# The second expert's first weights: packed values folded in by 64-row tiles and kept in HBM

## Chip, cores and metric

The kernel runs on one core of one Trainium2 chip. The metric is the time of one execution in device microseconds. Before the change it is 1086.9 us, the median of 3 runs (1085.64 to 1087.13).

## What is computed

```python
def sm_attn(qq, kk, vv):            # scale = 1/sqrt(64)
    a = softmax(scale * qq @ kk.T)
    return a @ vv
p_packed = sm_attn(p, k, v)         # 32 packed rows per head
x = sm_attn(q, p_packed, p_packed)  # 4 batches, 8 heads, 576 tokens, 64 wide
x = x as 2304 tokens x 512
out = 0
for e in range(4):                  # experts, weights w1[e] 512x1024, w2[e] 1024x512
    out += prob[:, e] * (relu(x @ w1[e]) @ w2[e])
out = (s * relu(out @ w_in)**2 + b) @ w_out
```

The second attention ends in a product of its weights a2 (tokens by 32 packed rows of each of 8 heads) with the packed values, and expert e begins with a product by w1[e]. The kernel multiplies the packed values into w1[e] first ("folds" them), so that per batch and expert one matrix of 256 rows (8 heads x 32) by 1024 columns stands in place of w1[e], and the expert reads a2 directly.

## The kernel before, in words

Numbers that must stay exact are kept in two parts, a high part (rounded to the fp32r type) and a low part (the rest), and each product is three matmuls: low x high, high x high, high x low.

After the first attention of batch 0 the main loop runs over 256 units, `ua`: expert e, batch bi, half hf of the batch's tokens, and one of 8 column blocks f. One turn i of the loop is called step i here. A batch is SB = 16 steps, an expert 64. In step i the loop first calls `run(i)`, which issues whatever was woven in at that step with `at(step, fn, ...)`, then `m1` for unit i + 2 (a2 times the folded first weights, L777, into a bank `h`; its relu is split by ScalarE, L798, and VectorE, L800), then `m2` for unit i (times w2, L823, into `acc`). So the order on every engine is written out by hand by the step numbers in the `at` calls (L1241 to L1284), and each engine works its list in order. SyncE (SP) issues nearly all DMAs, also in list order; a DMA that has to wait holds up those behind it.

Expert 0's weights are folded batch by batch out of the packed values `ptw` by `fold_w1`. Three forms of fold exist before the change:

- Expert 1 (the second): at steps 49 and 50 `pair_p` (L509) splits `ptw` into `ptph` and `ptpl`, laid out so that two batches lie on one 128 x 128 block. `load_w1` and `split_w1` bring and split w1[1] in four column groups. `fold_pair` (L613) then makes, for a pair of batches j, a column group c and x, six matmuls of 128 x 128 by 256 columns (L621), and ACT (L629) and DVE (L633) evict the two halves into `w1p` tiles in SBUF. j = 0 stands at steps 57 to 64, j = 1 at steps 89 to 96.
- Experts 2 and 3: at steps 91 and 93 `heads_p` (L526) gathers `pth` out of `ptph` and `ptpl`, eight POOL copies. `load_w1b`, `split_w1b` and `fold_heads` (L570) work on 64-row tiles: for a column half n, a row group gi and x, each of the three products is two matmuls with 64 rows and 512 columns, one for each half z of the partitions (L575), and ACT (L581) and DVE (L582) evict two banks into `w1o` tiles. `store_heads` (L590) writes them to `w1p_dram` in HBM, two DMAs of 512 KB a call. This is done for all four batches at once. `load_w1p` (L602) brings each batch's part back later, for each n and gi in four DMAs of 32 partitions.

What the tiles come from matters for the waits. `w1p` for even batches comes from 4 buffers of the pool `keep`, which expert 0 uses for its own folded weights until its last m1; `w1o` and the raw weights share 7 slots (`take`, `give`); the banks of a fold come from `ps_m`, 2 buffers; raw second weights come from 3 buffers, `load_w2` (L646) at steps 54 to 61 and `split_w2` (ACT L654, POOL L657) at steps 57 to 64 for expert 1.

The core of `fold_heads`, which the change calls for expert 1 too:

```python
for i, (a, w) in enumerate(((1, 0), (0, 0), (0, 1))):
    for z in range(2):
        r = slice(64 * z, 64 * z + 64)
        nc.tensor.matmul(
            ps[z], lhsT=pth[a][r, gi, x, :], rhs=w1s[e, n, gi][w][r, x, :],
            start=(i == 0), stop=(i == 2),
        )
```

Of the kernel before, what the change touches and what calls it, by code (L numbers as in the profile page):

```python
# [19 lines left out]
def attention_experts_mlp_kernel(  # L20
# [431 lines left out]
    def load_w1(e, c):  # L452
        if e == 0:
            t = keep.tile([P, KB, 256], F32, tag="w1", bufs=4, name=f"w1_{e}{c}")
        else:
            w1q[e, c], t = take([P, KB, 256], F32, f"w1r_{e}{c}")
        nc.sync.dma_start(
            out=t, in_=w1[e, :, c * 256 : (c + 1) * 256].rearrange("(r a) f -> a r f", a=P)
        )
        w1_t[e, c] = t  # L460
# [34 lines left out]
    def w1p_tile(e, bi, c):  # L495
        pool = wodd if bi % 2 else keep
        t = pool.tile([P, 2, G, 256], F32R, tag="w1p", bufs=4, name=f"w1p_{e}{bi}{c}")
        w1p[e, bi, c] = t[:, 0], t[:, 1]
        return w1p[e, bi, c]


    ptp, w1s = {}, {}
# [3 lines left out]
        for e in range(2, E)  # L506
    }

    def pair_p(j):  # L509
        if j == 0:  # L510
            for i, x in enumerate("hl"):
                ptp[i] = wf.tile([P, G, 2, 2, P], F32R, tag="ptp", bufs=2, name="ptp" + x)
        hi, lo = (ptp[i][:, :, :, j, :] for i in range(2))
        for bi in (0, 1):
            for y in range(2):
                r = slice(64 * y, 64 * y + 64)
                x = y ^ bi
                src = ptw[2 * j + bi][:, :, r]
                nc.scalar.activation(hi[:, :, x, r], src, AF.Copy)
                nc.gpsimd.tensor_tensor(  # L520
                    out=lo[:, :, x, r], in0=src, in1=f32(hi[:, :, x, r]), op=ALU.subtract
                )
# [3 lines left out]
    def heads_p(i):  # L526
        t = pth[i] = wf.tile([P, G, 2, P], F32R, tag="pth", bufs=2, name=f"pth{i}")
        for z in range(2):
            r = slice(64 * z, 64 * z + 64)
            for gi in range(G):  # L530
                nc.gpsimd.tensor_copy(
                    t[r, gi].rearrange("a x (j h r) -> a x j h r", j=2, h=2),
                    ptp[i][r, gi].rearrange("a x j (h z r) -> a z x j h r", h=2, z=2)[:, z ^ gi],
                )

    def split_w1(e, c, i):
        if i == 0:
            w1q["h", e, c], hi = take([P, KB, 256], F32R, f"w1h_{e}{c}")
            w1s[e, c] = (
                hi, keep.tile([P, KB, 256], F32R, tag="w1", bufs=4, name=f"w1l_{e}{c}")  # L540
            )
        hi, lo, raw = (x[:, 2 * i : 2 * i + 2] for x in (*w1s[e, c], w1_t[e, c]))
        nc.scalar.activation(hi, raw, AF.Copy)
        nc.vector.tensor_tensor(out=lo, in0=raw, in1=f32(hi), op=ALU.subtract)
        if i == 1:
            give(w1q[e, c])
# [61 lines left out]
    def w1p_block(e, bi, f, gi, x):  # L608
        if e == 1:
            return w1p[e, bi, f // 2][x][:, gi, (f % 2) * P : (f % 2 + 1) * P]  # L610
        return w1p[e, bi, f // 4, gi][:, x, (f % 4) * P : (f % 4 + 1) * P]

    def fold_pair(e, j, c, x):  # L613
        t = ps_m.tile([P, G, 256], F32, tag="m", name=f"pp1_{e}{j}{c}{x}")
        ph, pl = (ptp[i][:, :, :, j, :] for i in range(2))
        if j == 1 and x == 1:
            give(w1q["h", e, c])
        for gi in range(G):
            wh, wl = (w[:, 2 * gi + x] for w in w1s[e, c])
            for n, (a, w) in enumerate(((pl, wh), (ph, wh), (ph, wl))):  # L620
                nc.tensor.matmul(  # L621
                    t[:, gi, :], lhsT=a[:, gi, x, :], rhs=w, start=(n == 0), stop=(n == 2)
                )
        if x == 0:
            for bi in (2 * j, 2 * j + 1):
                w1p_tile(e, bi, c)
# [810 lines left out]
```

## Time and profile before

| | |
|---|---|
| median of 3 runs | 1086.9 us |
| the profiled execution | 1086.37 us |
| its span, first to last instruction | 1084.3 us |
| TensorE (PE) busy | 99% of the span |
| VectorE (DVE), ScalarE (ACT), GpSimd (POOL) busy | 62%, 42%, 18% |
| DMA moved | 170.23 MB, mean 157 GB/s |

The times are of the profiled execution; its span leaves out what lies before the first and after the last instruction. PE is the matmul stream, PEld the loading of its stationary operand, which runs beside it. SPq is the issue of DMAs by SyncE. A row of a timeline gives start, duration, engine, line, operation, output and input by the program's names, shapes and count, and in brackets the idle time before it and what ended that. Because matmuls overlap in the pipeline, the distance between starts, not the duration, is what one costs.

### The profile page before, as it was taken

Reading aid. Unit: us, or ns where it says so; the run is one execution under the profiler, and the core shown is the slowest. Engines: PE = TensorE matmul, PEld = TensorE weight load, DVE = VectorE, ACT = ScalarE, POOL = GpSimd, SP = SyncE. Lnnn points to the kernel's source line nnn. Section 1 sums busy time; section 2 is a strip of 40 time slices with the busy share of each in tenths; the row PEclk is TensorE's granted clock in tenths of the full one; section 3 lists DMA queues with packets and bytes.
Section 4 is the critical chain, followed back from the end, with each engine's and each line's share of the span. In section 5 each row is a group of like instructions: output and inputs, shape, how many; then the busy total and the mean of one; then the engine's idle time right before and its main releaser. Section 6 shows DMA issues by size and latency. Waiting matters only on the chain.

```text
span 1084.3 us, 16975 instructions
## 1 busy us (share of the span) xinstructions
PE 1069.9 (99%) x6263; PEld 914.9 (84%) x6263; DVE 676.4 (62%) x1298; ACT 450.1 (42%) x1014; POOL 195.3 (18%) x193
## 2 busy tenths in 40 slices
PE   8999999999999999999999999989999999999998
PEld 5777778888887888888888888878888888889887
DVE  7885754675575456465457645589845765775554
ACT  3533333553444343333435766665631332343111
POOL 1520212221110131010131122234201120210000
PEclk9999999999999999999999999999999999999999
DMA  9763320133036775575676242336856555665532
GB/s 285 177 114 69 69 89 1 40 107 115 32 103 223 226 216 159 182 216 172 207 192 191 73 126 88 134 139 242 330 187 216 185 208 172 217 209 184 183 113 88
DMA packets 102685, 170.23 MB, mean 157 GB/s; under 512 B 48185, under 2 KB 64825, under 8 KB 102603
## 3 DMA queue, kind: packets, MB, share of 16 engines
q1 hardware_dynamic: 101755, 168.04, 49.0%
q10 hardware_dynamic: 848, 1.11, 0.3%
q8 instruction: 50, 0.82, 0.3%
q14 instruction: 32, 0.26, 0.1%
HBM read 122.72 MB, written 46.40 MB: 156 GB/s over the span
## 4 chain that ended last, share of the span: by engine, by line
PE 92%; DVE 2%; ACT 2%; DMA 1%; issue 1%; SPq 1%; POOL 1%; ACTq 0%; DVEq 0%; POOLq 0%
PE acc L823 34%; PE h L777 18%; PE o L1018 18%; PE h L982 15%; PE pp L575 1%; PE pp L621 1%; DMA v<-in_v_dram 1%; PE pw L473 1%; PE pv L308 1%; PE s L375 0%; ACT xs L926 0%; PE tr L290 0%; PE warm L1068 0%; DMA q<-in_q_dram 0%; DVE xs L927 0%
## 5 line engine op out<-in xcount | busy, mean ns | idle before, releaser
L777 PEld LDWEIGHTS h<-a,w1p 128*128 128x128 f32 x1536 | 226.7, 188 | 33.2 <-issue 9.9
L777 PE MATMUL h<-a,w1p 128*128 128x320 f32 (+1 forms) x1536 | 250.6, 298 | 1.4 <-DVE rest L800 0.9
L1018 PE MATMUL o<-wo,gg 128*128 128x512 f32 x864 | 224.7, 394 | 2.0 <-DVE gg L950 2.0
L800 DVE SCALAR_TENSOR_TENSOR hl<-h,hh 128x256 fp32r<-128x256 f32 x256 | 107.9, 421 | 187.4 <-ACT rest L798 102.9
L982 PE MATMUL h<-xs,wop 128*128 128x384 f32 x1008 | 203.8, 338 | 1.5 <-DVE xt L844 1.5
L823 PE MATMUL acc<-w2l,hh 128*128 128x512 f32 x512 | 201.4, 393 | 0.5 <-POOL w2l L657 0.5
L823 PE MATMUL acc<-w2h,hh 128*128 128x512 f32 x512 | 201.5, 393 | 0.0
L823 PE MATMUL acc<-w2h,hl 128*128 128x512 f32 x512 | 200.3, 391 | 0.0
L982 PEld LDWEIGHTS h<-xs,wop 128*128 128x128 f32 x1008 | 180.9, 188 | 15.4 <-DVE xt L844 1.7
L1018 PEld LDWEIGHTS o<-wo,gg 128*128 128x128 f32 x864 | 160.1, 188 | 27.7 <-DVE gg L950 2.9
L798 ACT ACTIVATE hh<-h 128x256 fp32r<-128x256 f32 x256 | 97.3, 380 | 171.5 <-PE h L777 168.8
L823 PEld LDWEIGHTS acc<-w2h,hl 128*128 128x128 f32 x512 | 96.2, 188 | 21.7
L823 PEld LDWEIGHTS acc<-w2l,hh 128*128 128x128 f32 x512 | 96.4, 188 | 15.4 <-POOL w2l L657 0.7
L823 PEld LDWEIGHTS acc<-w2h,hh 128*128 128x128 f32 x512 | 96.4, 188 | 13.3
L936 ACT ACTIVATE yy<-yy 128x768 f32<-128x768 f32 x48 | 40.3, 839 | 112.9 <-DVE yy L1002 112.9
L1002 DVE TENSOR_TENSOR yy<-h,uv 128x384 f32<-128x384 f32 x96 | 51.0, 552 | 47.5 <-PE h L982 47.3
L946 ACT ACTIVATE gg<-yy,b_sb 128x768 fp32r<-128x768 f32 x48 | 44.8, 934 | 37.5 <-DVE yy L939 36.3
L950 DVE SCALAR_TENSOR_TENSOR gg<-yy,b_sb,gg 128x768 fp32r<-128x768 f32 x48 | 53.7, 1120 | 1.8 <-ACT gg L946 1.8
L657 POOL TENSOR_TENSOR w2l<-w2r,w2h 128x512 fp32r<-128x512 f32 x24 | 31.1, 1294 | 127.9 <-ACT w2h L654 104.5
L939 DVE SCALAR_TENSOR_TENSOR yy<-yy,s_sb 128x768 f32<-128x768 f32 x48 | 51.8, 1080 | 0.0
L1002 DVE TENSOR_TENSOR uv<-h,uv 128x384 f32<-128x384 f32 x48 | 26.4, 553 | 38.2 <-PE h L982 38.0
L1034 DVE TENSOR_TENSOR o_sb<-o,o_sb 128x512 f32<-128x512 f32 (+1 forms) x55 | 36.9, 673 | 16.7 <-PE o L1018 16.7
(399 smaller groups left out, 1146.9 us busy)
## 6 DMA issues: line engine op xcount, KB each, us to landing
xs<-xs_dram SPq DMA_DIRECT2D x63, 768.0 KB, 4.3
w1p_dram<-w1o SPq DMA_DIRECT2D x32, 512.0 KB, 3.7
w1p<-w1p_dram SPq DMA_DIRECT2D x128, 128.0 KB, 4.3
xs_dram<-xs SPq DMA_DIRECT2D x21, 768.0 KB, 3.5
w1r<-in_moe_w_dram SPq DMA_DIRECT2D x12, 512.0 KB, 4.8
w2r<-in_moe_w_dram SPq DMA_DIRECT2D x24, 256.0 KB, 3.8
out_dram<-o_sb SPq DMA_DIRECT2D x17, 256.0 KB, 2.0
v<-in_v_dram SPq DMA_DIRECT2D x8, 512.0 KB, 5.6
```

The lines of the kernel that those rows point to most:

```text
L777: nc.tensor.matmul(t[:, : width(bi, hf)], lhsT=w1p_block(e, bi, f, gi, w), rhs=a2[bi][:, x, gi, part(bi, hf)], start=(n == 0), stop=(n == ...
L798: nc.scalar.activation(hi, src, AF.Relu)
L800: nc.vector.scalar_tensor_tensor(out=lo, in0=src, scalar=0.0, in1=f32(hi), op0=ALU.max, op1=ALU.subtract)
L823: nc.tensor.matmul(acc[j], lhsT=x, rhs=w, start=(f == 0 and n == 0), stop=(g == NF - 1 and n == 2),)
L936: nc.scalar.activation(y, y, AF.Relu)
L939: nc.vector.scalar_tensor_tensor(out=y, in0=y, scalar=s_sb, in1=y, op0=ALU.mult, op1=ALU.mult)
L946: nc.scalar.activation(t[:, 0], y, AF.Identity, bias=b_sb)
L950: nc.vector.scalar_tensor_tensor(out=t[:, 1], in0=y, scalar=b_sb, in1=f32(t[:, 0]), op0=ALU.add, op1=ALU.subtract)
L982: nc.tensor.matmul(ps, lhsT=w[:, a, col], rhs=x[:, z, m, :], start=(n == 0), stop=(n == 3 * HK - 1),)
L1002: nc.vector.tensor_tensor(out=dst, in0=ps, in1=src, op=ALU.add)
L1018: nc.tensor.matmul(o_acc[i], lhsT=lhsT, rhs=w, start=(f == 0 and n == 0), stop=(f == FG - 1 and n == 2),)
L1034: nc.vector.tensor_tensor(out=dst[:, c], in0=acc[:, c], in1=dst[:, c], op=ALU.add)
```

## The change

Expert 1 takes the way of experts 2 and 3. `fold_pair`, `pair_p`, `split_w1` and `w1p_tile` go; `w1p_dram` gets an entry for expert 1; `load_w1` is left for expert 0 alone. The packed values are gathered anew: `heads_pick` copies them from `ptw` by POOL, 16 copies of 64 partitions x 32 at step 33 and 16 at step 41, into `p_pick`, a free part of the tile that holds the rows of the expert probabilities; `heads_p`, at step 48, then splits them by one ACT and one DVE instruction. `heads_p` at steps 91 and 93 goes. For expert 1, `split_w1b` stands at steps 50 to 57, `fold_heads` one step later, `store_heads` two steps later, one call in every step; `load_w1p` for its first batch at steps 57, 58, 61 and 62, for the others as experts 2 and 3 have it (the first four steps of the batch before).

```diff
-        if e == 0:
-            t = keep.tile([P, KB, 256], F32, tag="w1", bufs=4, name=f"w1_{e}{c}")
-        else:
-            w1q[e, c], t = take([P, KB, 256], F32, f"w1r_{e}{c}")
+        t = keep.tile([P, KB, 256], F32, tag="w1", bufs=4, name=f"w1_{e}{c}")
...
-        for e in range(2, E)
+        for e in range(1, E)
     }
...
+    def heads_pick(j):
+        t = p_pick.rearrange("a (g x j h r) -> a g x j h r", g=G, x=2, j=2, h=2)
         for z in range(2):
             for gi in range(G):
+                for h in range(2):
+                    for x in range(2):
+                        r = 64 * h + 32 * (z ^ gi)
+                        nc.gpsimd.tensor_copy(
+                            t[half(z), gi, x, j, h], ptw[2 * j + (x ^ h)][half(z), gi, r : r + 32]
+                        )
...
+    def heads_p():
+        for i in range(2):
+            pth[i] = wf.tile([P, G, 2, P], F32R, tag="pth", bufs=2, name=f"pth{i}")
+        hi, lo = (pth[i].rearrange("a g x c -> a (g x c)") for i in range(2))
+        nc.scalar.activation(hi, p_pick, AF.Copy)
+        nc.vector.tensor_tensor(out=lo, in0=p_pick, in1=f32(hi), op=ALU.subtract)
...
     def w1p_block(e, bi, f, gi, x):
-        if e == 1:
-            return w1p[e, bi, f // 2][x][:, gi, (f % 2) * P : (f % 2 + 1) * P]
         return w1p[e, bi, f // 4, gi][:, x, (f % 4) * P : (f % 4 + 1) * P]
...
                 for c in range(4):
-                    if ne == 1 and nb % 2 == 0:
-                        for x in range(2):
-                            at(s0 + 9 + 2 * c + x, fold_pair, ne, nb // 2, c, x)
-                for c in range(4):
                     n, gi = divmod(c, 2)
-                    if ne > 1:
-                        d = c if nb else (6, 7, 13, 14)[c]
+                    if ne:
+                        d = c if nb else ((6, 7, 13, 14) if ne > 1 else (9, 10, 13, 14))[c]
                         at(s0 + d, load_w1p, ne, nb, n, gi)
-                    if bi != B - 1 or ne < 2:
+                    if bi != B - 1:
                         continue
                     for x in range(2):
                         k = 2 * c + x
-                        if n:
+                        if ne == 1:
+                            d = s0 + 2 + k
+                        elif n:
                             d = s0 + 2 * k - 7
...
                         if x == 0:
-                            at(d - 4, load_w1b, ne, n, gi)
+                            at(max(d - 4, s0) if ne == 1 else d - 4, load_w1b, ne, n, gi)
                         at(d, split_w1b, ne, n, gi, x)
                         at(d + 1, fold_heads, ne, n, gi, x)
-                        at(d + 3, store_heads, ne, n, gi, x)
+                        at(d + (2 if ne == 1 else 3), store_heads, ne, n, gi, x)
                 if bi == B - 1:
-                    for c in range(4 if ne == 1 else 0):
-                        at(s0 + (0, 1, 5, 7)[c], load_w1, ne, c)
-                        for i in range(2):
-                            at(s0 + 3 + 2 * c + i, split_w1, ne, c, i)
...
-        for j in range(2):
-            at((B - 1) * SB + 1 + j, pair_p, j)
-            at((B + 1) * SB + 11 + 2 * j, heads_p, j)
+        at(2 * SB + 1, heads_pick, 0)
+        at(2 * SB + 9, heads_pick, 1)
+        at((B - 1) * SB, heads_p)
```

The order of the instructions shows three places. First SP's list from expert 1's first weights to the raw weights of the last layers (w1r: raw first weights, w2r: raw second weights, wi0raw: raw weights of the last layers), before:

```order
L457 DMA w1r_2506<-in_moe_w_dram 128x4x256
L646 DMA w2r_2532<-in_moe_w_dram 128x512
L457 DMA w1r_2558<-in_moe_w_dram 128x4x256
L646 DMA w2r_2560<-in_moe_w_dram 128x512
L646 DMA w2r_2585<-in_moe_w_dram 128x512
...
L646 DMA w2r_2772<-in_moe_w_dram 128x512
L678 DMA wi0raw<-in_moe_w_in_dram 128x4x256
```

and with the change, from the third block of second weights to the last load of expert 1's first batch:

```order
L595 DMA w2r_2702<-in_moe_w_dram 128x512
L573 DMA w1p_2724<-w1p_dram_90 32x1024 x4
L561 DMA w1p_dram_90<-w1o_2692 128x1024
L561 DMA w1p_dram_90<-w1o_2695 128x1024
L595 DMA w2r_2751<-in_moe_w_dram 128x512
L573 DMA w1p_2772<-w1p_dram_90 32x1024 x4
...
L595 DMA w2r_2845<-in_moe_w_dram 128x512
L573 DMA w1p_2864<-w1p_dram_90 32x1024 x4
L595 DMA w2r_2873<-in_moe_w_dram 128x512
L627 DMA wi0raw<-in_moe_w_in_dram 128x4x256
L573 DMA w1p_2894<-w1p_dram_90 32x1024 x4
```

Where only second weights stood, the last stores (L561) and the loads of the first batch (L573) now stand between them.

On PE, the first fold of expert 1 with the m1 (h) behind it, at step 57 of the kernel before:

```order
L621 MATMUL pp_1000_2607<-w1h_2452,ptpl 128x256
L621 MATMUL pp_1000_2607<-w1h_2452,ptph 128x256
L621 MATMUL pp_1000_2607<-w1l_2453,ptph 128x256
L621 MATMUL pp_1000_2607<-w1h_2452,ptpl 128x256
L621 MATMUL pp_1000_2607<-w1h_2452,ptph 128x256
L621 MATMUL pp_1000_2607<-w1l_2453,ptph 128x256
L777 MATMUL h_2630<-a_3_2198,w1p_2219 128x256 x3
L777 MATMUL h_2630<-a_3_2198,w1p_2221 128x256 x3
```

and the first fold of expert 1 with the change, at step 51:

```order
L546 MATMUL pp_10000_2477<-w1h_2449,pth_2397 128x512
L546 MATMUL pp_10001_2478<-w1h_2449,pth_2397 128x512
L546 MATMUL pp_10000_2477<-w1h_2449,pth_2396 128x512
L546 MATMUL pp_10001_2478<-w1h_2449,pth_2396 128x512
L546 MATMUL pp_10000_2477<-w1l_2450,pth_2396 128x512
L546 MATMUL pp_10001_2478<-w1l_2450,pth_2396 128x512
L726 MATMUL h_2493<-a_3_2231,w1p_2359 128x320 x3
```

One call fills two banks (pp_10000 and pp_10001) in place of one, eight calls stand in place of sixteen, and they begin six steps earlier.

On POOL, the second attention of batch 3 (sc: its scores, a: its weights a2), with the change:

```order
L405 TENSOR_TENSOR sc_2147<-sc_2147,mx_2161 128x16x32
L419 TENSOR_TENSOR sc_2084<-sc_2084,r_300_2164 128x20x32
L508 COPY raw_3_96<-ptw_83 64x32 x16
L419 TENSOR_TENSOR sc_2147<-sc_2147,r_310_2227 128x16x32
L439 TENSOR_TENSOR a_3_2231<-at_2204,a_3_2231 128x2x320
```

The 16 copies of the second gathering (into raw_3, the tile that holds p_pick) have come between the two products L419; before, the two stood next to each other.

## Rows read from the trace of the kernel before

**Rows 1.** The page, part 1: busy time, share of the span, instructions.
```profile
PE 1069.9 (99%) x6263; PEld 914.9 (84%) x6263; DVE 676.4 (62%) x1298; ACT 450.1 (42%) x1014; POOL 195.3 (18%) x193
```
**Rows 2.** The page, part 4: chain that ended last, shares by line.
```profile
PE acc L823 34%; PE h L777 18%; PE o L1018 18%; PE h L982 15%; PE pp L575 1%; PE pp L621 1%; DMA v<-in_v_dram 1%; PE pw L473 1%; PE pv L308 1%; PE s L375 0%; ACT xs L926 0%; PE tr L290 0%; PE warm L1068 0%; DMA q<-in_q_dram 0%; DVE xs L927 0%
```
**Rows 3.** Timeline of PE, m1 groups: start us, duration us, what.
```profile
199.70 0.88 PE L777 MATMUL h<-a,w1p 128*128 128x256 f32 x6
...
222.39 0.88 PE L777 MATMUL h<-a,w1p 128*128 128x256 f32 x6
...
224.50 0.88 PE L777 MATMUL h<-a,w1p 128*128 128x256 f32 x6
...
280.87 0.87 PE L777 MATMUL h<-a,w1p 128*128 128x256 f32 x6
...
303.37 0.88 PE L777 MATMUL h<-a,w1p 128*128 128x256 f32 x6
...
305.47 0.88 PE L777 MATMUL h<-a,w1p 128*128 128x256 f32 x6
```
**Rows 4.** DMA view of the stretch 158.8 to 218 us.
```profile
DMA packets 1396, 2.15 MB, mean 36 GB/s; under 512 B 112, under 2 KB 624, under 8 KB 1392
```
**Rows 5.** Timeline of PE around a fold of expert 2.
```profile
318.23 1.04 PE L777 MATMUL h<-a,w1p 128*128 128x320 f32 x6
...
320.49 1.04 PE L777 MATMUL h<-a,w1p 128*128 128x320 f32 x6
...
323.74 1.15 PE L777 MATMUL h<-a,w1p 128*128 128x320 f32 x6
...
326.11 1.04 PE L777 MATMUL h<-a,w1p 128*128 128x320 f32 x6
```
**Rows 6.** Timeline of ACT and DVE behind that fold.
```profile
323.84 1.09 ACT L581 ACTIVATE w1o<-pp 128x512 fp32r<-128x512 f32 x2 [1.72 <-PE pp L575]
324.48 1.29 DVE L582 TENSOR_TENSOR w1o<-pp,w1o 128x512 fp32r<-128x512 f32 x2 [0.71 <-ACT w1o L581]
```
**Rows 7.** Timeline of POOL, 161 to 168 us, and of PE behind it.
```profile
161.18 1.27 POOL L419 TENSOR_TENSOR sc<-sc,r 128x640 f32<-128x640 f32 x1
164.80 1.05 POOL L419 TENSOR_TENSOR sc<-sc,r 128x512 f32<-128x512 f32 x1 [2.35 <-DVE r L417]
165.81 1.57 POOL L439 TENSOR_TENSOR a<-at,a 128x640 fp32r<-128x640 f32 x1
...
170.75 1.04 PE L777 MATMUL h<-a,w1p 128*128 128x320 f32 x6
```
**Rows 8.** Groups of POOL by form: busy us, mean ns, idle before.
```profile
L195 POOL COPY pbd<-pT 32x128 f32<-32x128 f32 x4 | 1.1, 286 | 0.9 <-DVE pT L1073 0.8
```
**Rows 9.** Timeline of step 57: m1, and ACT's write that waits for it.
```profile
202.51 0.88 PE L777 MATMUL h<-a,w1p 128*128 128x256 f32 x6
203.07 0.59 ACT L629 ACTIVATE w1p<-pp 64x512 fp32r<-64x512 f32 x1 [2.08 <-PE h L777]
```
**Rows 10.** DMA view of 384.2 to 396.1 us: loads of folded weights alone.
```profile
DMA packets 1074, 2.83 MB, mean 238 GB/s; under 512 B 323, under 2 KB 323, under 8 KB 1072
```
**Rows 11.** DMA view of 377.5 to 379.5 us, then of 358.9 to 361.4 us.
```profile
DMA packets 221, 0.82 MB, mean 410 GB/s; under 512 B 19, under 2 KB 19, under 8 KB 221
...
DMA packets 239, 0.91 MB, mean 365 GB/s; under 512 B 16, under 2 KB 16, under 8 KB 239
```
**Rows 12.** Line L602, the loads of folded weights: issue to landing.
```profile
DMA to landing us min/median/max: 3.0/4.3/7.5
```
**Rows 13.** Timeline of ACT at the boundary to expert 2.
```profile
388.63 0.63 ACT L654 ACTIVATE w2h<-w2r 128x512 fp32r<-128x512 f32 x1 [1.97 <-DMA w2r<-in_moe_w_dram]
```
**Rows 14.** Line L646, the loads of second weights: issue ns, then landing.
```profile
L646 SPq DMA_DIRECT2D w2r<-in_moe_w_dram x24: 327/336/1756, 149.0 to 543.5; - x24
...
DMA to landing us min/median/max: 2.5/4.2/7.9
```
**Rows 15.** The page, part 5: POOL's part of the split of second weights.
```profile
L657 POOL TENSOR_TENSOR w2l<-w2r,w2h 128x512 fp32r<-128x512 f32 x24 | 31.1, 1294 | 127.9 <-ACT w2h L654 104.5 <-PE pp L621 22.5 <-DMA w2r<-in_moe_w_dram 0.8
```

More of the change, by code (lines that the diff above doesn't have):

```diff
@@ L493, in fold_lo @@
             )
[L495 to L502, printed above, removed]
+    w1s = {}
     w1p_dram = {
         e: dram.tile([2, 2, P, 2, G, 2 * HF], F32, name=f"w1p_dram{e}")
-        for e in range(2, E)
+        for e in range(1, E)
     }
[L509 to L522, printed above, removed]
@@ L524, in attention_experts_mlp_kernel @@
     pth = {}
-    def heads_p(i):
-        t = pth[i] = wf.tile([P, G, 2, P], F32R, tag="pth", bufs=2, name=f"pth{i}")
+    def heads_pick(j):
+        t = p_pick.rearrange("a (g x j h r) -> a g x j h r", g=G, x=2, j=2, h=2)
         for z in range(2):
-            r = slice(64 * z, 64 * z + 64)
             for gi in range(G):
[L531 to L546, printed above, removed]
+                for h in range(2):
[4 more added lines that the diff above has]
+                        )
@@ L608, in w1p_block @@
     def w1p_block(e, bi, f, gi, x):
-        if e == 1:
-            return w1p[e, bi, f // 2][x][:, gi, (f % 2) * P : (f % 2 + 1) * P]
         return w1p[e, bi, f // 4, gi][:, x, (f % 4) * P : (f % 4 + 1) * P]
[L613 to L626, printed above, removed]
-        for y in range(2):
-            r = half(y)
-            nc.scalar.activation(w1p[e, 2 * j + (y ^ x), c][0][r], t[r], AF.Copy)
-        for y in range(2):
-            r = half(y)
-            hi, lo = w1p[e, 2 * j + (y ^ x), c]
-            nc.vector.tensor_tensor(out=lo[r], in0=t[r], in1=f32(hi[r]), op=ALU.subtract)
     raw_t = {}
     *raw0, p_rows = (
-        keep.tile([P, NS, DM], F32, tag="x2", bufs=XB, name=f"raw0_{i}")[:, 0] for i in range(4)
+        keep.tile([P, NS, DM], F32, tag="x2", bufs=XB, name=f"raw0_{i}") for i in range(4)
     )
+    raw0 = [t[:, 0] for t in raw0]
+    p_rows, p_pick = p_rows[:, 0], p_rows[:, 1]
     def load_w2(e, f):
```

## The prediction

> **What bounds the kernel now.** I read the page's first part, then the chain of waits, then TensorE's timeline, then the DMA views. The first part shows TensorE busy for 99% of the span [rows 1]. A busy share can hide waiting, so the chain comes next: four TensorE lines make 34 + 18 + 18 + 15 = 85% of the span, and the two folds of first weights, L575 and L621, 1% each [rows 2]. In the timeline the reader should look at the start times of consecutive m1 groups, because the distance between two of them is one step of the main loop (called step i below: m1 of unit i+2, m2 of unit i, then the woven work of step i+1). Plain 256-column steps are 2.11 us or 2.10 us apart and no step around the change is longer than its matmuls explain [rows 3]. So TensorE is the bound here, any matmul time removed comes back one for one, and any new wait of TensorE costs in full. The DMA views say how much room there is beside it: from 158.8 to 218 us, where the change puts its new transfers, the queues move 36 GB/s on average [rows 4].
>
> **The change, part by part.**
>
> *Removed: 16 calls of fold_pair (L621).* The first eight stand in the steps that start at 199.70 and end at 222.39: 22.69 us, less eight plain steps of 2.10, leaves 5.9 us. The second eight, 280.87 to 303.37, are 22.50 us, less 16.80: 5.7 us. Together **11.6 us** [rows 3].
>
> *Added: 8 calls of fold_heads for expert 1.* The same calls exist for experts 2 and 3. The two steps from 320.49 to 326.11 hold one of them and take 5.62 us; two plain steps of this width take 2 x 2.26 (318.23 to 320.49). So one call costs 1.10 us: 0.99 in its own step, 0.11 in the next [rows 5]. Eight calls: **8.8 us**. Below, the bound is the streaming of three pairs alone: L823's 34% of 1084.3 us for its 1536 matmuls of 512 columns is 0.24 us each [rows 2], 0.72 us a call. Above, a call in every step instead of every second one may cost a few tenths more. I keep 1.10, the only row of this very shape.
>
> The Trainium skill, TensorEngine Tiling (Array Packing), states under "Theoretical Speedup" up to 2x for a contraction of at most 64 rows, and under "Key Properties" that changing the tiling mode drains the engine. By the full 2x the eight calls would take the streaming bound, an estimate of 5.8 us in place of 8.8; the 1.10 us of [rows 5] sides with the drain.
>
> So matmul work falls by 11.6 - 8.8 = **2.8 us**.
>
> *ACT and DVE.* 32 evictions on each become 16; the splitting of the weights (8 and 8) keeps its count and stays at steps 50 to 57. The new density is in steps 51 to 58: after a fold, ACT needs 1.09 us for both banks, DVE ends at 324.48 + 1.29 = 325.77, which is 2.03 us after the start of the m1 behind the fold at 323.74 [rows 5, 6]. The next fold needs both banks. Steps 51 to 55 are longer (three accumulators), steps 56 and 57 give it 2.10 us plus the 0.11: cover of 0.1 to 0.2 us. If it is gone, two or three waits of a few tenths; I cost it at nothing and put it in the upper end. The eight ACT and eight POOL instructions of pair_p go, one ACT and one DVE instruction of heads_p come at step 48, two steps ahead of need: nothing.
>
> *POOL.* heads_pick adds 16 copies of 64x32 at step 33 and 16 at step 41. The second lot stands between the L419 that ends at 162.45 and the L419 at 164.80, which waits for DVE: 2.35 us are free there. Behind it the low part of a2[3] ends at 167.38 and its first reader is the m1 at 170.75: 3.4 us more [rows 7]. The nearest copy, 32x128, takes 0.286 us [rows 8]; 16 of them are 4.6 us, under the 5.7 us of cover. Cost nothing; above 0.36 us per copy it would start to show.
>
> *SP and the DMA queue: the term that decides.* SP gets 16 stores of 512 KB (8.4 MB out) and 64 loads of 128 KB (8.4 MB back). For the last half of expert 0 they are tight. The first four loads overwrite a slot of expert 0, so SP waits with them for m1 of step 57: before, the ACT write into such a slot waited for the same m1 until 203.07, 0.56 us after its start [rows 9]. Behind them in SP's order stand, up to the last load that expert 1's first batch needs: 16 loads in all, 6 stores, 5 blocks of second weights of 256 KB, one raw block of 512 KB. That last load must have landed for the gi=1 half of the m1 in step 66. The time given is step 57 (2.10 + 1.10), step 58 (2.10 + 0.11) and steps 59 to 65 (7 x 2.10), 20.1 us, less 0.56, plus about 0.3 for the first half of that m1: **19.9 us**. The time needed: in a stretch with such loads alone the queue ran at 238 GB/s, so 16 x 0.131 MB take 8.8 us [rows 10]; 6 stores, 5 blocks and the raw block at 410 GB/s take 7.7 + 3.2 + 1.3 us [rows 11]; the fastest landing of a load is 3.0 us, of which 0.55 is its own transfer, so 2.4 us of lead [rows 12]. That is 23.4 us, 3.5 too many. By the mixed stretch instead (365 GB/s over 7.1 MB [rows 11]) it is 19.4 + 2.4 = 21.8 us, 1.9 too many. I take the middle, **2.7 us** of new TensorE wait, since the queue here is a mixture, though one richer in loads than that stretch. Lower end 0: all at 410 GB/s, 17.3 + 2.4 = 19.7 us. Upper end 5.5: the first working plus 2 us in which SP is held up by POOL's release of a raw buffer, the size of the longer wait for second weights that ACT already shows [rows 13].
>
> The later loads (expert 1's batches 1 to 3) have twelve steps or more to land: nothing.
>
> *Sum.* The profiled execution took 1086.37 us, 0.5 under the median of the runs shown and inside their spread; 1086.37 - 2.8 + 2.7 = **1086.3 us**. For this kernel 0.2% is 2.2 us, about what a measurement can tell from no change.
>
> **The rivals.**
>
> *The transfers are hidden.* Wait under 0.6 us, so the 2.8 us arrive: 1083.6 to 1084.2. For it: the queue is almost empty before, and the boundary to expert 2 has a similar crowd with no step lengthened. Against it: that boundary has half as many stores in the last steps, and even there ACT waited 1.97 us for a block of second weights [rows 13]. Chance 0.25.
>
> *The second weights come late in a circle.* A block f can be asked for only when POOL has finished block f-3, because there are three raw buffers. One turn is landing + ACT 0.63 + POOL 1.29 + issue 0.34 us, for three steps of 6.3 us; it holds the pace up to a landing of 4.0 us, and the median is 4.2 [rows 13 to 15]. ACT works in order, so m1's relu (hh) stands behind a late block, and TensorE behind hh. With the longest landing seen, 7.9 us, a turn is 10.2 us, 3.4 us per step, and blocks 3 to 7 cost 5 x 1.3 = 6.5 us in place of the 2.7: 1090.1 us. From 5.7 us of landing on it is slower than before, from 7.0 us on by over 0.2%. For it: stores and loads ahead of each block in one queue. Against: the median lies only just above the 4.0, and ACT's queue has two steps of lead. Chance 0.16.
>
> *The halves of a fold overlap fully and nothing drains.* Each call at the streaming bound, 0.72 us: 3.0 us under the forecast, 1083.3. It is the full speedup that the Trainium skill, TensorEngine Tiling (Array Packing), gives under "Theoretical Speedup". Against it stands the step with L575 [rows 5]. Chance 0.02. That the change does not do what it says I leave without a chance: both forms are read in the trace.
>
> **How the numbers follow.** The forecast (wait between 0.6 and 5.0 us, 1084.2 to 1088.6) has 0.57; its own range is 1084.2 to 1088.6. Faster by over 0.2%: 0.25 + 0.02 = 0.27. Same: 0.57. Slower by over 0.2%: 0.16. The range takes in the hidden case from 1083.6 and the near part of the circle up to 1089.5; the far circle and the full overlap, some 0.14, lie outside.
>
> **What would show it.** L621's steps gone from 200 to 222 and from 281 to 303 us, and every step there back at 2.1; eight steps from about 182 us on longer by 1.1; then one to three gaps of TensorE within steps 62 to 66 (about 217 to 230 us), ended by a load of w1p or by hl behind a late w2h, 2 to 3 us in total; the DMA share near full from step 57 to 66. POOL's copies under 0.3 us with no step near 165 us lengthened. I am wrong if the gaps are missing (hidden case), if ACT's waits for w2r add up to more than TensorE's waits for w1p and exceed 5 us (circle), or if a fold costs other than 1.10.

## The result, and the profile after

The changed kernel takes 1092.76 us (median of 12 runs, 1088.03 to 1096.32), the kernel before 1086.56 us (12 runs on the same chip, 1085.64 to 1088.12): ratio 1.0055, 95% interval 1.0043 to 1.0066. It is **slower by 6.2 us**, above the range that the prediction gave (1084.2 to 1088.6). The profiled execution took 1090.52 us with a span of 1088.7 us, 4.4 us more than the span before.

The first part of the page and the chain of waits of the changed kernel, to be laid beside [rows 1, 2]:

```profile
PE 1070.1 (98%) x6215; PEld 908.5 (83%) x6215; DVE 663.1 (61%) x1283; ACT 437.9 (40%) x991; POOL 193.9 (18%) x209
...
PE acc L772 34%; PE o L967 18%; PE h L726 18%; PE h L931 15%; PE pp L546 2%; DMA w1p<-w1p_dram 1%; DMA v<-in_v_dram 1%; PE pv L308 1%; DMA w2r<-in_moe_w_dram 1%; PE pw L470 1%; POOL w2l L606 0%; DMA k<-in_k_dram 0%; PE s L375 0%; ACT xs L875 0%; PE tr L290 0%
```

TensorE is busy for as long as before, although the change takes matmul work away: some of its work has become slower. Two transfers now stand in the chain, the loads of folded weights (w1p) and of second weights (w2r). Neither was there in [rows 2].

TensorE's timeline of the changed kernel, the m1 groups (m1 is L726 here, L777 before): start us, duration us, what, and in brackets the idle time of TensorE before and what ended it.

```profile
153.29 1.14 PE L726 MATMUL h<-a,w1p 128*128 128x320 f32 x6
...
182.86 1.04 PE L726 MATMUL h<-a,w1p 128*128 128x320 f32 x6
...
215.23 0.88 PE L726 MATMUL h<-a,w1p 128*128 128x256 f32 x6
...
221.58 0.98 PE L726 MATMUL h<-a,w1p 128*128 128x256 f32 x6
225.79 0.98 PE L726 MATMUL h<-a,w1p 128*128 128x256 f32 x6 [1.85 <-DVE hl L749]
229.42 1.39 PE L726 MATMUL h<-a,w1p 128*128 128x256 f32 x6 [0.34 <-DVE hl L749]
232.04 0.86 PE L726 MATMUL h<-a,w1p 128*128 128x256 f32 x6
234.13 0.51 PE L726 MATMUL h<-a,w1p 128*128 128x256 f32 x3
236.49 0.59 PE L726 MATMUL h<-a,w1p 128*128 128x256 f32 x3 [1.85 <-DMA w1p<-w1p_dram]
239.25 1.47 PE L726 MATMUL h<-a,w1p 128*128 128x256 f32 x6
241.96 0.88 PE L726 MATMUL h<-a,w1p 128*128 128x256 f32 x6
...
292.08 0.88 PE L726 MATMUL h<-a,w1p 128*128 128x256 f32 x6
308.91 0.88 PE L726 MATMUL h<-a,w1p 128*128 128x256 f32 x6
346.14 1.15 PE L726 MATMUL h<-a,w1p 128*128 128x320 f32 x6
```

The same two ends, the 41st and the 113th m1 group, in the kernel before:

```profile
152.81 1.14 PE L777 MATMUL h<-a,w1p 128*128 128x320 f32 x6
...
340.60 1.15 PE L777 MATMUL h<-a,w1p 128*128 128x320 f32 x6
```

These 72 steps hold everything that the change touches on TensorE. They take 346.14 - 153.29 = 192.85 us, before 340.60 - 152.81 = 187.79: 5.06 us more. (The rest of the difference of the spans is a wait of 0.94 us at 571.89 us that only the profiled execution of before has, and small differences at the start.) Six steps, from 221.58 to 241.96 with one plain one among them, account for it: 20.38 us less one plain 2.09 leaves 18.29 for five steps of 2.10, an excess of **7.8 us**. All else in the 72 steps is 2.7 us shorter. Of the excess the brackets name 1.85 + 0.34 + 1.85 = **4.0 us** of idle time. The other half is not a wait. The windows of TensorE there show what it is (stretch, its length, PE busy and matmuls, granted clock, DMA share, GB/s):

```profile
224.00:226.00 2.00, 0.21 (x1) 1.00 1.02 379
226.00:228.00 2.00, 2.00 (x10) 0.73 1.08 320
228.00:230.00 2.00, 1.67 (x5) 0.50 0.99 234
230.00:232.00 2.00, 2.00 (x11) 0.91 1.10 314
...
234.00:236.00 2.00, 0.64 (x5) 1.00 0.97 231
236.00:238.00 2.00, 1.51 (x7) 0.79 1.04 234
238.00:240.00 2.00, 2.00 (x8) 0.50 1.14 265
240.00:242.00 2.00, 2.00 (x11) 0.85 1.01 225
```

After each of the two long gaps the granted clock falls to 0.50, the lower of TensorE's two levels (1.2 of 2.4 GHz), and both times the matmuls run at full pace again 4 to 5 us after the gap has ended (from 230.64 and 240.80 us on). Busy time times the missing share of clock, window by window (0.54 + 0.83 + 0.18, then 0.32 + 1.00 + 0.30), gives **3.2 us**. The last 0.6 us of the excess the rows don't split. The DMA share is near 1 throughout.

Behind the first two gaps stand the second weights. ACT's waits from 180 to 262 us (us in total, times, longest), and its timeline there:

```profile
ACT w2h L603 <- DMA w2r<-in_moe_w_dram: 11.8, 5, 3.6
```

```profile
220.16 0.63 ACT L603 ACTIVATE w2h<-w2r 128x512 fp32r<-128x512 f32 x1 [3.63 <-DMA w2r<-in_moe_w_dram]
224.38 0.63 ACT L603 ACTIVATE w2h<-w2r 128x512 fp32r<-128x512 f32 x1 [3.31 <-DMA w2r<-in_moe_w_dram]
228.00 0.63 ACT L603 ACTIVATE w2h<-w2r 128x512 fp32r<-128x512 f32 x1 [2.73 <-DMA w2r<-in_moe_w_dram]
```

ACT runs in order, so the relu (hh) of the next m1 stands behind a late block, DVE's hl behind hh, and TensorE's second matmuls behind hl. [Rows 13] had one such wait of 1.97 us with nobody late behind it; here five follow each other, the longest three shown. SP's timeline shows the order in which the queue is fed (x is the number of issues, the duration that of all of them):

```profile
210.50 2.04 SPq L573 DMA_DIRECT2D w1p<-w1p_dram  x4
212.64 0.84 SPq L561 DMA_DIRECT2D w1p_dram<-w1o  x2
213.65 0.71 SPq L595 DMA_DIRECT2D w2r<-in_moe_w_dram  x1
214.45 3.16 SPq L573 DMA_DIRECT2D w1p<-w1p_dram  x4
217.71 0.84 SPq L561 DMA_DIRECT2D w1p_dram<-w1o  x2
...
228.01 6.79 SPq L573 DMA_DIRECT2D w1p<-w1p_dram  x8
```

Loads of folded weights, stores and second weights alternate, and each is issued only after those ahead of it. POOL, last, where the second lot of copies stands (against [rows 7]):

```profile
162.87 2.59 POOL L508 COPY raw<-ptw 64x32 f32<-64x32 f32 x16
165.54 1.05 POOL L419 TENSOR_TENSOR sc<-sc,r 128x512 f32<-128x512 f32 x1
```

### The profile page after: what moved, and what is told of

It is laid out like the page before. It is cut to its first block, busy times and chain, and to the rows that moved or that the text cites. A ratio compares the mean times of both kernels' runs of the same rounds, so it can differ in the third digit from the quotient of the medians.

```text
span 1088.7 us, 16981 instructions
## 1 busy us (share of the span) xinstructions
PE 1070.1 (98%) x6215; PEld 908.5 (83%) x6215; DVE 663.1 (61%) x1283; ACT 437.9 (40%) x991; POOL 193.9 (18%) x209
## 4 chain that ended last, share of the span: by engine, by line
PE 90%; DMA 3%; DVE 2%; ACT 2%; issue 1%; SPq 1%; POOL 1%; ACTq 0%; DVEq 0%; POOLq 0%
PE acc L772 34%; PE o L967 18%; PE h L726 18%; PE h L931 15%; PE pp L546 2%; DMA w1p<-w1p_dram 1%; DMA v<-in_v_dram 1%; PE pv L308 1%; DMA w2r<-in_moe_w_dram 1%; PE pw L470 1%; POOL w2l L606 0%; DMA k<-in_k_dram 0%; PE s L375 0%; ACT xs L875 0%; PE tr L290 0%
## 5 line engine op out<-in xcount | busy, mean ns | idle before, releaser
L726 PEld LDWEIGHTS h<-a,w1p 128*128 128x128 f32 x1536 | 228.3, 189 | 40.9 <-issue 11.5
L726 PE MATMUL h<-a,w1p 128*128 128x320 f32 (+1 forms) x1536 | 252.8, 300 | 4.5 <-DVE hl L749 2.5
L772 PEld LDWEIGHTS acc<-w2h,hl 128*128 128x128 f32 x512 | 96.7, 189 | 21.8
L553 DVE TENSOR_TENSOR w1o<-pp,w1o 128x512 fp32r<-128x512 f32 x48 | 30.9, 686 | 43.9 <-ACT w1o L552 43.9
```

The source lines that it names most:

```text
L726: nc.tensor.matmul(t[:, : width(bi, hf)], lhsT=w1p_block(e, bi, f, gi, w), rhs=a2[bi][:, x, gi, part(bi, hf)], start=(n == 0), stop=(n == ...
L772: nc.tensor.matmul(acc[j], lhsT=x, rhs=w, start=(f == 0 and n == 0), stop=(g == NF - 1 and n == 2),)
```

## The experiments

My theory after the result: the queue of transfers is crowded from some 200 to 245 us, whichever consumer comes next in it is late, and each long gap costs TensorE more than its length, because the clock falls behind it. The rivals: the circle of three buffers for second weights, the way the transfers are issued, and a saving of matmul work that is not there. Each experiment is the changed kernel with the edit shown; the kernel before ran beside each of them (medians 1087.34 us with the first four, 1087.02 with the next four, 1086.98 with the ninth and tenth, 1087.1 with the last). For each I also give the length of the 72 steps. 185.09 us, what the last experiment took without any wait, is the floor; what is above it is the cost of gaps.

### 1. Second weights loaded early

```diff
-            raw = wf.tile([P, DM], F32, tag="raw", bufs=3, name=f"w2r_{e}{f}")
+            raw = wf.tile([P, DM], F32, tag="raw", bufs=7, name=f"w2r_{e}{f}")
...
-                        at(s0 + 6 + f, load_w2, ne, f)
+                        at(s0 + (6 + f if ne > 1 or f == 7 else 0), load_w2, ne, f)
```

> Seven raw buffers, and expert 1's second weights (blocks 0 to 6) asked for at step 48, ahead of every store. Crowd theory (the DMA engines have more bytes to move between step 57 and the first m1 of expert 1's second column half than time): 1.3 MB leave the crowded stretch, ACT's waits for second weights fall from 11.8 us to under 1, and the wait for the last folded weights shrinks by about 3 us, so to nothing: 1082.5 to 1085 us. Circle theory (a block can only be asked for when POOL frees one of three raw buffers, and the lateness feeds on itself): the three gaps behind late second weights go with what the lower clock cost there, some 4 us, but the 3 us at the wait for folded weights stay: 1086 to 1088 us.

Measured: 1088.54 us, ratio 1.0016 (1.0001 to 1.0032); 72 steps in 188.92 us. The gaps behind hl are gone. One is left in TensorE's timeline, and its step takes 5.25 us:

```profile
232.96 0.59 PE L726 MATMUL h<-a,w1p 128*128 128x256 f32 x3 [2.17 <-DMA w1p<-w1p_dram]
```

So two delays had been there, and this one can be taken away alone. As a choice between the two expectations the run fits the circle better: the time is 0.5 us above its range and 3.5 us above that of the crowd, and the wait for the folded weights stayed, as the circle had it. More buffers and earlier loads came together here; the next experiment parts them.

### 2. Seven buffers, the same load steps

```diff
-            raw = wf.tile([P, DM], F32, tag="raw", bufs=3, name=f"w2r_{e}{f}")
+            raw = wf.tile([P, DM], F32, tag="raw", bufs=7, name=f"w2r_{e}{f}")
```

> Seven raw buffers and nothing else: the second weights are asked for at the same places of SP's list, but SP no longer waits there for POOL. Circle theory: the gaps behind second weights go, about 4 us gained, 1086 to 1088.5 us. Crowd theory: the blocks still lie behind the stores in the same queue, under 1 us gained, 1090 to 1093 us.

Measured: 1092.49 us, ratio 1.0044 (1.0029 to 1.0059); 72 steps in 191.94 us. ACT still waits 9.1 us for second weights, and TensorE has gaps in the same places (1.85, 0.34 and 1.85 us in the changed kernel):

```profile
226.49 0.98 PE L726 MATMUL h<-a,w1p 128*128 128x256 f32 x6 [1.68 <-DVE hl L749]
230.81 1.07 PE L726 MATMUL h<-a,w1p 128*128 128x256 f32 x6 [1.95 <-DVE hl L749]
237.74 0.59 PE L726 MATMUL h<-a,w1p 128*128 128x256 f32 x3 [0.56 <-DMA w1p<-w1p_dram]
```

With four more buffers no block has to wait for POOL's release of block f-3, and nothing that the measurement can tell is won. The circle falls, and the time is where the crowd had it (1090 to 1093 us). What helped in experiment 1 was the place of the blocks in the queue.

### 3. Expert 1's stores issued by ACT

```diff
-            nc.sync.dma_start(
+            (nc.scalar if e == 1 else nc.sync).dma_start(
```

> Expert 1's 16 stores are issued by ACT instead of SP; the bytes and their steps stay. Crowd theory by bytes: the same 16 DMA engines move them, so the waits stay within 1 to 2 us of the changed kernel, 1090 to 1093 us. Order theory (SP's list and its in-order waits hold the loads back, not the bytes): loads and second weights no longer stand behind stores, the waits go, 1083 to 1086 us.

Measured: 1090.01 us, ratio 1.0021 (1.0012 to 1.003); 72 steps in 190.66 us. It lies at the lower end of what the crowd by bytes was to give and 4 us above the other theory. ACT's waits for second weights stay (10.0 us). TensorE's first long gap is now one behind w1p (1.69 us at 225.05), new ones of 0.79 and 0.22 us stand from 251.12 on behind DVE, and all five of its waits add up to 4.0 us, as much as in the changed kernel. What the profiled execution lacks is the lower clock: it is 1.00 in every window of 2 us from 220 to 256 us. So the waits do not come from who issues the stores. The Trainium skill, DMA: Bandwidth & Descriptors (Rules for kernel authors), says that spreading transfers over issuing engines brings no bandwidth, only issue time; the waits for second weights, 10.0 us here and 11.8 before the edit, agree.

### 4. The folds two steps earlier

```diff
-                            d = s0 + 2 + k
+                            d = s0 + k
...
-                            at(max(d - 4, s0) if ne == 1 else d - 4, load_w1b, ne, n, gi)
+                            at(s0 if ne == 1 and k < 6 else d - 4, load_w1b, ne, n, gi)
```

> Expert 1's splits, folds and stores all two steps earlier, the rest as in the changed kernel. Crowd theory: the last three pairs of stores leave some 7 us earlier, the stretch from step 57 on has about 1 pair less ahead of the loads and second weights land in time: waits under 1 us, 1082.5 to 1086 us. Circle theory: the raw buffers turn as before, the gaps behind second weights stay at 3 us or more: 1087 to 1091 us.

Measured: 1089.48 us, ratio 1.002 (1.0005 to 1.0035); 72 steps in 191.15 us. The time is in the circle's range and above the crowd's, but the circle's sign, gaps of 3 us or more behind second weights, is missing: two waits of 0.67 and 0.93 us are left, both behind w1p (224.00 and 233.64 us), and a later consumer is hit instead:

```profile
250.59 1.11 PE L726 MATMUL h<-a,w1p 128*128 128x320 f32 x6 [1.90 <-DVE rest L749]
```

DVE was held up there for 4.3 us by raw weights of the layer behind the experts (wi2raw), whose load stands in SP's order behind batch 1's loads. The crowd had only been moved on.

### 5. Both moves together

The edits of experiments 1 and 4, and batch 0's loads at steps 8, 9, 11 and 12:

```diff
-                        d = c if nb else ((6, 7, 13, 14) if ne > 1 else (9, 10, 13, 14))[c]
+                        d = c if nb else ((6, 7, 13, 14) if ne > 1 else (8, 9, 11, 12))[c]
```

> Both moves together: the second weights' loads early (seven raw buffers), the eight folds and their stores two steps earlier, and batch 0's loads of first weights at steps 8, 9, 11 and 12 of their sixteen instead of 9, 10, 13 and 14. Theory (a queue crowded for some 30 us, each delay of TensorE followed by a stretch at its lower clock): each of the two moves left one gap, in other places (5.25 us between two starts of first matmuls with the loads early, behind w1p; 1.90 us at 250.6 us with the folds early, behind the expert weights wi2raw that stand after batch 1's sixteen loads). Together they should clear the w1p gap and leave at most the one behind wi2raw: 1084 to 1086.5 us, ratio to before 0.998 to 1.000. Rival (the folds themselves cost more than read, or the ones removed saved less than 11.6 us, and the gaps only cover that up): no faster than 1087 us even without gaps in the rows.

Measured: 1087.53 us, ratio 1.0004 (0.9994 to 1.0014), a miss: 1 us above what was expected, and not to be told from before. 72 steps take 188.74 us. The wait behind w1p is gone, but the eighth block of second weights, still loaded behind batch 0's loads, is late (ACT waits 4.3 us for it, TensorE 0.55 us behind hl at 231.33). The raw weights of the last layers, next in the queue, are late too: a gap of 1.22 us at 234.92 stands behind DVE's wait for wi0raw (1.0 us), and 0.58 us at 248.82 behind its wait for wi2raw. With gaps left, the rival is not answered by this run.

### 6. Batch 1's loads spread

```diff
-                        d = c if nb else ((6, 7, 13, 14) if ne > 1 else (8, 9, 11, 12))[c]
+                        d = 3 * c + 2 if ne == nb == 1 else c if nb else ((6, 7, 13, 14) if ne > 1 else (8, 9, 11, 12))[c]
```

> As the kernel with both moves, and batch 1's four tiles are loaded at steps 2, 5, 8 and 11 of the sixteen before they are read, instead of 0 to 3, so that the loads of the expert weights (wi raw) don't stand behind 64 issues in SP's queue. Theory: no wait of TensorE for w1p, w2r or DVE's rest above 0.3 us is left between 185 and 260 us, granted clock 1.000, so the step's saving of the sum shows by itself: 1086.6 - 2.8 = 1083.8 us (1083.2 to 1084.8), ratio 0.9975, interval wholly below 1. Rival (the sum's saving isn't there): same within 0.1% of before or slower with all waits gone.

Measured: 1084.47 us, ratio 0.9979 (0.997 to 0.9988): **faster than before**. The clock is 1.000. Two gaps are left where none above 0.3 us was expected, of 0.56 us (w1p at 223.22) and 0.67 us (hl at 232.16), and the 72 steps take 187.10 us, 2.0 above the floor. The rival, that the matmul saving isn't there, falls.

### 7. One gap made on purpose

On the kernel of experiment 6:

```diff
-            nc.scalar.activation(w2_t[e, f][0], raw_t[e, f], AF.Copy)
+            for _ in range(8 if (e, f) == (1, 3) else 1):
+                nc.scalar.activation(w2_t[e, f][0], raw_t[e, f], AF.Copy)
```

> As the kernel with both moves and batch 1 spread, and ACT makes the same copy (the high part of one block of second weights, 0.6 us each) eight times instead of once, at one step near 208 us; what is computed is the same. ACT is 4.2 to 4.4 us late there; TensorE's second matmuls are about a step behind, so it should wait some 2 to 2.5 us once, with no queue of transfers near it. Theory (a gap of about 2 us is followed by a stretch at the lower of TensorE's two clock levels, whatever made the gap): the time rises over the kernel without the copies by more than the wait in the rows, by 1.5 to 4 us more, and a 2 us window behind the gap shows a granted clock near 0.5: some 5 us in all. Rival (the lower clock belongs to the crowded transfers): the time rises by the wait alone, 2 to 2.5 us, and the granted clock stays at 1.00.

Measured: 1086.93 us, ratio to before 0.9996 (0.9986 to 1.0005), 2.46 us above experiment 6. TensorE's timeline holds this one gap, at 224 us and not near 208, and no other; then the windows behind it:

```profile
224.40 1.47 PE L727 MATMUL h<-a,w1p 128*128 128x256 f32 x6 [1.89 <-DVE hl L750]
228.15 0.88 PE L727 MATMUL h<-a,w1p 128*128 128x256 f32 x6
```

```profile
222.00:224.00 2.00, 0.51 (x3) 1.00 1.04 422
224.00:226.00 2.00, 1.60 (x7) 0.66 1.03 258
226.00:228.00 2.00, 2.00 (x6) 0.50 1.00 229
228.00:230.00 2.00, 2.00 (x12) 0.99 1.04 289
```

The 72 steps take 188.71 us, 3.6 above the floor, for 1.89 us of idle time. So a gap that ACT's arithmetic made, not a transfer, draws the lower clock too, and costs 1.9 times its length. The total of 5 us that I expected was too high, since experiment 6's own two gaps (2.0 us) were gone in this execution. By the medians alone the rise of 2.46 us would also fit the rival's 2 to 2.5; it is the clock of 0.50 that speaks against it.

The queue was full beside the gap here as well. Experiment 4 shows the same away from transfers: behind its gap of 1.90 us at 250.59 the clock falls while the DMA share is 0.00:

```profile
252.00:254.00 2.00, 2.00 (x6) 0.50 0.00 0
254.00:256.00 2.00, 2.00 (x9) 0.66 0.00 0
```

### 8. Whole-tile loads

```diff
-        for p in range(4):
+        if e == 1:
+            nc.sync.dma_start(
+                out=f32(t).rearrange("a x f -> a (x f)"),
+                in_=w1p_dram[e][bi % 2, bi // 2, :, n, gi],
+            )
+        for p in range(4 if e > 1 else 0):
```

> The changed kernel with one edit: each of expert 1's sixteen tiles of first weights is loaded by one transfer of 128 rows from one place instead of four of 32 rows from four places (the same bytes; it reads rows of other tokens' weights, so it leaves out the picking of rows). Theory A (the form of the loads makes the crowd: 32-row transfers ran at 238 GB/s, transfers of all rows at 365 to 410 GB/s): batch 0's loads take 5.1 to 5.8 us of queue instead of 8.8, SP issues 16 instead of 64 in place of some 36 us of issues, and the waits behind w1p go; those behind w2r fall to below half (ACT's 11.8 us to under 5). Time 1085 to 1088 us. Theory B (the crowd is the order of SP's queue, the stores ahead of the loads): the waits behind w2r stay at 9 to 12 us as they start at 217 us, when four loads of first weights have been issued; the time stays above 1090 us.

Measured: 1087.96 us, ratio 1.0011 (1.0002 to 1.002); 72 steps in 189.17 us. Each theory has half: the time is A's, but ACT's waits for second weights (10.1 us) and the first gap (2.04 us behind hl) are B's. What went is the rest: the wait behind w1p shrinks to 0.71 us, and the clock stays at 1.00 in every window here. The DMA view of a stretch with loads, 236 to 244 us of the changed kernel, then 236 to 242 us of this one:

```profile
DMA packets 1031, 1.92 MB, mean 240 GB/s; under 512 B 184, under 2 KB 693, under 8 KB 1030
```

```profile
DMA packets 939, 2.15 MB, mean 358 GB/s; under 512 B 74, under 2 KB 453, under 8 KB 938
```

The queue moves 240 GB/s with four loads of 32 rows a tile and 358 with one of 128. The Trainium skill, SBUF — State Buffer (Door 1: The DMA port swizzle), explains that a transfer to 32 neighbouring partitions reaches half of the ports; 240 beside 358 goes that way, though both stretches hold other transfers too.

### 9. The eighth block of second weights earlier

On experiment 6:

```diff
-                        at(s0 + (6 + f if ne > 1 or f == 7 else 0), load_w2, ne, f)
+                        at(s0 + (6 + f if ne > 1 else 11 if f == 7 else 0), load_w2, ne, f)
```

> As the kernel with both moves and batch 1 spread, and the eighth block of second weights is loaded at step 11 instead of 13, ahead of batch 0's loads of first weights in SP's queue. Theory: that block came too late (ACT's copy waited 4.4 us for it, TensorE 0.83 and 0.38 us behind it); its wait goes and only the one of 0.8 us behind w1p at 223 us is left or moves: 1.0 to 1.3 us less than the kernel without it, 1083.2 to 1083.6 us where before is 1087.0, ratio 0.9965 to 0.997. Rival (the block's 256 KB ahead of the loads push those back by as much as it gains): w1p's wait grows by 0.6 us or more and the time stays within 0.4 us of 1084.5.

Measured: 1084.40 us, ratio 0.998 (0.9972 to 0.9989). The time is the rival's: the 1083.2 to 1083.6 us expected are missed, and the medians of this run and experiment 6 can't be told apart. But the rival's sign is missing too, since TensorE no longer waits for w1p at all. The 72 steps take 186.32 us, 0.8 less than in experiment 6, with one gap of 1.05 us behind hl at 234.85; behind it stands DVE's wait of 1.44 us for wi0raw, the next load in the queue.

### 10. The other pool of tiles

On experiment 9:

```diff
-        pool = wodd if bi % 2 else keep
+        pool = wodd if (bi + (e == 1)) % 2 else keep
...
-                        d = 3 * c + 2 if ne == nb == 1 else c if nb else ((6, 7, 13, 14) if ne > 1 else (8, 9, 11, 12))[c]
+                        d = 3 * c + 2 if ne == nb == 1 else c if nb else ((7, 8, 10, 11), (9, 10, 13, 14), (6, 7, 13, 14))[ne - 1][c]
```

> As the last, and expert 1's even batches take the first-weight tiles of the other pool, odd ones those of this: batch 0's tiles are then free when its loads are issued (steps 7, 8, 10 and 11), where they waited for expert 0's last batch, whose tiles they took, until 212 us; expert 2's batch 0 has that wait instead, and its loads go at steps 9, 10, 13 and 14. Theory (crowd of the queue between the folds' end and batch 0's reads): with the loads from 200 us on, nothing waits at 210 to 240 us: 1082.5 to 1083.5 us, ratio 0.996. Rival: the collision of tiles moves to the start of expert 2 at 420 us, and that start, whose second weights go at the same steps as the change's did, shows waits behind w2r and w1p and a lower clock of its own: 1085 to 1091 us, with 2 to 7 us of gaps between 418 and 450 us.

Measured: 1084.70 us, ratio 0.9978 (0.9968 to 0.9988). Both are half right. The 72 steps take 185.08 us and no wait is listed in them, but at the start of expert 2, where the collision now is, four steps are 1.5 us too long, among them:

```profile
393.17 0.59 PE L726 MATMUL h<-a,w1p 128*128 128x256 f32 x3 [0.54 <-DMA w1p<-w1p_dram]
```

### 11. The same for expert 2

On experiment 10:

```diff
-                        at(s0 + (6 + f if ne > 1 else 11 if f == 7 else 0), load_w2, ne, f)
+                        at(s0 + (6 + f if ne > 2 else 11 if f == 7 else 0), load_w2, ne, f)
...
-                        d = 3 * c + 2 if ne == nb == 1 else
+                        d = 3 * c + 2 if ne < 3 and nb == 1 else
```

> As the last, and expert 2 gets what expert 1 has: its second weights' first seven blocks at the head of the sixteen steps, the eighth at step 11, its batch 1's tiles at steps 2, 5, 8 and 11. In the run before this one the collision that moved to expert 2 cost 1.49 us between 383 and 395 us (steps of 2.29, 2.20, 2.43 and 2.97 us in place of 2.10), and nothing waited at 205 to 262 us. Theory: with the queue cleared there too, no step between 380 and 400 us is over 2.2 us, and 1.5 us go: 1083.0 to 1083.8 us where before is 1087.0, ratio 0.9965 to 0.997. Rival (the start of expert 2 is bound by tiles that come free late, not by the queue): those four steps keep an excess of 1 us or more, and the time stays within 0.4 us of 1084.5.

Measured: **1083.30 us** (1082.56 to 1085.01), ratio **0.997** (0.9958 to 0.9981), the fastest of all. TensorE waits for nothing from 180 to 262 us, nor from 370 to 400. The two ends of the 72 steps, then three windows of TensorE:

```profile
153.19 1.14 PE L726 MATMUL h<-a,w1p 128*128 128x320 f32 x6
...
338.28 1.15 PE L726 MATMUL h<-a,w1p 128*128 128x320 f32 x6
```

```profile
200.00:214.00 14.00, 14.00 (x80) 1.00 1.02 351
214.00:220.00 6.00, 6.00 (x36) 1.00 0.80 244
220.00:224.00 4.00, 4.00 (x24) 1.00 1.05 318
```

185.09 us in place of 187.79. The queue is about as full as in the changed kernel, but from some 200 to 224 us in place of 216 to 245, and from 180 to 262 us no engine's wait is put down to a load. A full queue without a gap leaves the clock at 1.00.

## Why the prediction was wrong

**Matmul work (8.8 added, 11.6 removed, net -2.8): right.** Experiments 10 and 11 have the folds and no gap, and their 72 steps are 187.79 - 185.08 = 2.71 and 2.70 us shorter than before. In the changed kernel the eight steps that held fold_pair, 292.08 to 308.91, take 16.83 us where [rows 3] had 22.50. By the up to 2x that the Trainium skill, TensorEngine Tiling (Array Packing), gives under "Theoretical Speedup" the calls would have cost some 3 us less (an estimate). The trace sides again with the fold at 1.10 us: the nine steps from 182.86 to 215.23 hold the eight calls and take 32.37 us, where plain ones of the same widths take 23.6 (four of 2.94, two of 2.78, three of 2.10), so a call costs 1.09 us.

**POOL, ACT and DVE at nothing: right.** The second sixteen copies took 2.59 us, 0.16 each, against the cover of 5.7; the waiting L419 came at 165.54 in place of 164.80 [rows 7], of which 0.48 us is the later start of this execution, and the steps around it did not grow: from 160.48 to 174.12 us before and from 160.96 to 174.60 after, 13.64 us both times.

**The queue, "the term that decides": right in its place and in the queue as the cause, wrong in what it costs.** The crowd, the full DMA share, the gaps behind hl and behind w1p are where the prediction put them. The step that failed is the sum's new wait of 2.7 us: it measured 7.8. Three things were missing.

- *"Any new wait of TensorE costs in full"*: it costs more. The idle time was 4.0 us, inside the ends of 0 and 5.5, and another 3.2 us went to matmuls at the lower clock behind the gaps. No row read before the prediction showed the lower clock: the mean granted clock of that execution is 1.000, and TensorE had no gap of this length near the change. Experiment 7 prices it with one gap: 1.89 us of idle time, 3.6 us of loss.
- *One deadline*: the working asked when the last load of 16 lands. The second weights in the same queue have deadlines of their own, ahead of it. ACT waited for them five times and TensorE twice behind hl; these gaps and the one behind w1p add up, as experiment 1 shows by taking the first away and leaving the other.
- *The queue's own time*: the working needed 21.8 to 23.4 us from the first load to the last and gave 19.9. From the issue of the first load at 210.50 us to the m1 half that waited for the last, at 236.49, it is 26.0. That the wait for w1p is 1.85 us and not some 6 (an estimate: 26.0 less 19.9) comes from the earlier gaps, which had already put this m1 back by 4.2 us (three steps from 221.58 to 232.04 us, 10.46 in place of 6.3).

With the measured cost of a gap, 1.9 times its length, the term's 2.7 us would have been 5 us and the forecast about 1088.7 us (an estimate), on the slow side but still 4 us short of the measured median.

**The rivals.** "The transfers are hidden" is false for the change and true for experiment 11. "The circle" gave 1090.1 us, near the profiled 1090.52, and the sign that I had named for it (ACT's waits for second weights over 5 us and over TensorE's for w1p) came up, 11.8 against 1.9 us. Experiment 2 shows that it is not the cause all the same: the sign did not tell a late queue from a late buffer.

**What stays open.** The median of the changed kernel lies 2.2 us above its profiled execution, so that execution shows only a part of the loss; what the others add, more or longer gaps or something else, no trace here shows. And experiment 11 gains 3.8 us by the medians, of which the 72 steps explain 2.7; the wait of 0.94 us at 571.89 us, which the profiled execution of before has and none of the changed kernel's, may be a part of the rest.

## What to carry to other kernels

A transfer that is added to a queue must be judged by every consumer behind it, each with its own time limit, and not by the last; taking one delay away uncovers the next until the whole stretch is spread out, as experiments 1, 4, 5 and 6 did in turn. Where TensorE is the bound, price a gap of about 2 us at up to twice its length, since the clock fell behind most such gaps here. And a saving that a profile proves is worth pursuing through the waits that come with it: the same folds were 0.55% slower and then 0.3% faster by the times at which folds, stores and loads were issued and the buffers that let them go so early.

## What was not expected of the hardware

- The fall of the clock did not follow every gap. In experiment 8 a gap of 2.04 us left the granted clock at 1.00, in experiment 7 one of 1.89 us brought it to 0.50 for some 3 us. Of the nine gaps over 1.6 us in these traces from 150 us on the clock fell behind six (1.85 twice, 1.89, 1.90, 1.95 and 2.17 us) and stayed at 1.00 behind three (1.68, 1.69 and 2.04 us). What decides between them is not shown.
- The start of the program varies by itself: the 41st m1 group comes at 152.81 us before, 153.29 in the changed kernel, 155.35 in experiment 10, though the change puts no work ahead of it but sixteen copies on POOL. In experiment 10 the granted clock was 0.85 and 0.80 in the two stretches of 5 us from 15 to 25 us, where it is 1.00 before. That is as large as the effects looked for here, and why the length of the 72 steps told more than the span.
